# A fused Fourier-mixing and SwiGLU kernel: PSUM banks and work buffers handed out by the build-time planner, a table of unit kinds, and gates seeded by ScalarE

## The chip, the cores and the metric

The kernel runs on one core of one Trainium2 chip. The metric is device microseconds of one execution. A core has four engines that compute: TensorE (PE in the profile, its weight loads PEld), VectorE (DVE), ScalarE (ACT) and GpSimd (POOL). SyncE (SP) issues most of the transfers. Each engine runs its own list of instructions in order, and semaphores tie the lists together.

## The reference: what is computed

The input `x` has 8 sequences of 3008 rows and 256 columns. Its two-dimensional Fourier transform is taken (over rows, then over columns), the real part is kept, and each of the 24064 rows goes through a SwiGLU block with 1536 hidden columns:

```python
X = np.fft.fft(x, axis=1); X = np.fft.fft(X, axis=2); x = X.real
g = x @ w_gate                       # 256 -> 1536
silu = g * (1.0 / (1.0 + np.exp(-g)))
val = x @ w_val
return (silu * val) @ w_out          # 1536 -> 256
```

## The kernel before, in words

**Symmetry.** The transform of a real sequence at row M-k mirrors that at row k. So the kernel works on half of the rows, 12032 of them, as columns of two matrices: an even part P (tile `Pt`) and an odd part Q (`Qt`). For a column, the gate of row k is `Wp·P + Wq·Q` and that of its mirror row is `Wp·P - Wq·Q`; the same holds for the value. The transform over the 256 columns is folded into the weights (`Wp`, `Wq`), so only the transform over rows is done on data: GpSimd folds the loaded rows of a sequence (lines 158 to 182), TensorE multiplies them by tables of sines and cosines (`transform_op`), ScalarE copies one result out (`od`), and VectorE adds and subtracts to fill `Pt` and `Qt` (line 1345).

**Tiles and units.** The columns are cut into 24 tiles, most of them 512 wide (`wide`). A unit is a tile and one of 12 blocks of 128 hidden columns, so there are 288 units. For each unit, the gate and the value of the plus row and of the mirror row are formed in two PSUM banks, one for `g` and one for `v`, and turned into two products, `hp` (plus) and `hm` (mirror), in bf16. There are several kinds of unit:

- *Whole* units (18, in the first tiles): TensorE forms plus with `Wp·P + Wq·Q`, and then adds `Wm·Q` with `Wm = -2·Wq`, so that the same bank holds the mirror. That is three matmuls each for gate and value. Silu is ScalarE's, both products are VectorE's (`whole_a`, `whole_b`).
- *Ordinary* units: the gate as above in three matmuls, but the value in two. The value's even part is taken out of the bank after the first matmul (`es`); after the second one the bank holds the plus value, and VectorE makes the mirror as `2·es - v` (line 1124). The Q part lacks a term in its first row, and a copy of that row is spread over all partitions by two transfers per tile (`br`, `bc`). VectorE adds it, times a weight per partition (`w0`), while it takes the even part out (line 1063).
- *Seeded* values (`SEED`): ScalarE writes `bc` times `w0` into the bank before the first matmul (line 1012), the matmuls add to it, ScalarE copies the even part out (line 1061), and the last matmul uses `Wm` (by then rescaled to `-Wq`) in place of `Wq`.
- *Split* gates (`GATE`): the gate too is done in two matmuls, with the even part by VectorE (line 1042) and the mirror by VectorE (line 1102).
- *Pool* products (`POOL_END`): ScalarE copies the value out of the bank (line 1140) and GpSimd multiplies (line 1143), in place of VectorE (line 1134).

GpSimd multiplies the mirrors of two units at a time, from a buffer `sv` that holds silu and value side by side (line 1131). When a tile's 12 units are done, its `hp` and `hm` are multiplied with `Wo` during the next tile (`OWork`, 96 matmuls of 256 columns for a full tile), ScalarE copies each pair of results into an `ev` buffer (line 1186), and SP stores it.

**What sets the order.** Nothing in the steady part is written in its final order. Each piece of work is handed to `Sched.add` with its engine, an estimated duration, what it reads and writes, and the buffers that it opens. `Sched.run` then plays the engines forward: at each step it takes, within a window per engine, the piece that can start first by those estimates, and at the end it emits all instructions in that order. Buffers come from pools: PSUM 3 banks for `g`, 3 for `v`, 2 for output and transforms; in SBUF 3 each for `sp`, `sg` and `ev`, 2 each for `sv`, `es` and `od`. A pool hands out its buffers in the order in which they are asked for. The estimates before are, for instance:

```python
def pe_us(n):   return (n + 6) / 2400
def act_us(n):  return n / 1200 + 0.055
def dve_us(n):  return n / 960 + 0.072
```

Of the kernel before, what the change touches and what calls it, by code (L numbers as in the profile page):

```python
# [12 lines left out]
F32 = mybir.dt.float32  # L13
# [14 lines left out]

@with_exitstack
def kernel(
# [47 lines left out]
    odp = ctx.enter_context(tc.tile_pool(name="od", bufs=2))  # L80
# [3 lines left out]
    ctx.enter_context(tc.manual_schedule())  # L84

    Wp = const.tile([P, 2, Dff], BF16, name="Wp")
# [135 lines left out]
    SC = tq.tile([P, 2, 2, 2, D], F32, name="SC")  # L222
    SA = tp.tile([P, 2, 4, 2, D], F32, name="SA")
# [472 lines left out]
    sgp = ctx.enter_context(tc.tile_pool(name="sg", bufs=3))  # L696
    spp = ctx.enter_context(tc.tile_pool(name="sp", bufs=3))
    svp = ctx.enter_context(tc.tile_pool(name="sv", bufs=2))
    esp = ctx.enter_context(tc.tile_pool(name="es", bufs=2))
    brp = ctx.enter_context(tc.tile_pool(name="br", bufs=1))  # L700
    bcp = ctx.enter_context(tc.tile_pool(name="bc", bufs=2))
    evp = ctx.enter_context(tc.tile_pool(name="evO", bufs=3))
# [26 lines left out]

    ROW_GAP = 1  # L730
# [4 lines left out]
    ES_BUFS = 2  # L735
    SP_BUFS = 3
    SG_BUFS = 3
    EV_BUFS = 3
    W_PE = 2.0
    W_ACT = 2  # L740
    W_DVE = 3
    W_POOL = 6.0
    SH_SEED = -0.5
    SH_EG = 0.5
    SH_SP = 0.0
    SH_ES = 0.5
    SH_GM = 0.0
    SH_SM = 0.0
    SH_VM = 0.0
    SH_VAL = 0.0  # L750
    SH_HP = 1
    SH_HM = -0.5
    SH_EV = 0.5
    SH_FOLD = -2
    SH_OD = 0.0
    SH_PUT = -1
    GRP = 4
    WM_ACT = ((1, 0), (1, 1))
    class Op:
        __slots__ = ("eng", "dur", "lat", "fn", "at", "n", "deps", "owners", "new", "start", "end", "users")  # L760

    LAG = {"DMA": 0.0, "PE": 0.20, "ACT": 0.17, "DVE": 0.15, "POOL": 0.12, "SP": 0.0}
    BUFS = {"g": 3, "v": 3, "o": 2, "sp": SP_BUFS, "sv": 2, "es": ES_BUFS, "sg": SG_BUFS, "ev": EV_BUFS, "od": 2, "h": 2, "bc": 2, "br": 1, "pq": 5, "cp": 2,
            "fc": 1, "st": 3}
    WINDOW = {"PE": W_PE, "ACT": W_ACT, "DVE": W_DVE, "POOL": W_POOL, "SP": 3.0, "DMA": 1e9}
    PSUM = ("g", "v", "o")

    class Sched:

        def __init__(self):  # L770
            self.ops = []
            self.wr, self.rd = {}, {}
            self.live = {p: [] for p in BUFS}
            self.clock = 0.0

# [3 lines left out]
        def add(self, eng, dur, fn, r=(), w=(), new=(), lat=None, shift=0.0):  # L779
            o = Op()  # L780
            o.eng, o.dur, o.fn, o.n = eng, dur, fn, len(self.ops)
            o.lat = LAG[eng] if lat is None else lat
            o.at = self.clock + shift
            if eng == "PE":
                self.clock += dur
            o.new, o.deps, o.owners = list(new), set(), set()
            for k in r:
# [4 lines left out]
                if k[0][0] in PSUM:  # L792
                    o.deps.update(x for x in same if self.ops[x].eng != eng)
                same.append(o.n)
            for k in w:
# [4 lines left out]
                self.wr[k] = o.n  # L800
            o.deps.discard(o.n)
# [3 lines left out]
        def run(self, begin):  # L805
            ops = self.ops
            last, queue = {}, {p: [] for p in BUFS}
            for o in ops:
                for w_ in o.owners:
                    if w_[0] in BUFS:  # L810
                        last.setdefault(w_, set()).add(o.n)
                for w_ in o.new:
                    if w_ not in queue[w_[0]] and w_ not in self.live[w_[0]]:
                        queue[w_[0]].append(w_)
            free = {p: [0.0] * (BUFS[p] - len(self.live[p])) for p in BUFS}
            owned = {w_ for p in BUFS for w_ in self.live[p]}
# [3 lines left out]
            for l in todo.values():  # L820
                l.sort(key=lambda o: (o.at, o.n))
            t_eng = {e: begin.get(e, 0.0) for e in todo}
# [3 lines left out]
            for o in ops:  # L826
                o.end = None

            def ready(o):
                at = 0.0  # L830
                for d in o.deps:
                    x = ops[d]
                    if x.end is None:
                        return None
                    at = max(at, x.end + (x.lat if x.eng != o.eng or x.eng == "SP" else 0.0 if x.eng == "PE" else 0.03))
                for w_ in o.new:
# [3 lines left out]
                    if queue[p][0] != w_ or not free[p]:  # L840
                        return None
                    at = max(at, min(free[p]))
                return at

            while left:
                best = None
                floor = min(l[0].at for l in todo.values() if l)
                for e, l in todo.items():
                    if not l:
                        continue  # L850
                    pick = None
                    for o in l[:60]:
                        if o.at > l[0].at + WINDOW[e]:
# [4 lines left out]
                        s = max(at, t_eng[e], lanes[0] if e == "SP" else 0.0)  # L858
                        if pick is None or s < pick[0] - 0.01:
                            pick = (s, o)  # L860
                        if s <= t_eng[e]:
# [717 lines left out]
```

## Time and profile before

| | |
|---|---|
| three runs | 612.43, 613.17, 614.85 us; median 613.17 |
| span of the profiled execution, first to last instruction | 610.2 us |
| the profiled execution's own time | not listed; its span lies 3.0 us under the median of the runs and 2.2 under the fastest |
| granted TensorE clock | 1.000 |
| busy: PE, DVE, ACT, POOL | 601.1, 580.9, 525.3, 473.8 us |
| HBM traffic | 29.43 MB read, 24.65 MB written |

The groups that the change touches, each with its count, busy time and mean duration from the page:

```profile
L1131 POOL TENSOR_TENSOR hm<-sv 128x1024 bf16<-128x1024 f32 (+2 forms) x135 | 251.3, 1862 | 111.7 <-ACT sv L1110 61.6
L1134 DVE TENSOR_TENSOR hp<-sp,v 128x512 bf16<-128x512 f32 (+2 forms) x264 | 177.4, 672 | 5.6 <-ACT sp L1107 3.9
L1012 ACT ACTIVATE v<-bc,w 128x512 f32<-128x512 bf16 (+2 forms) x126 | 87.4, 694 | 0.2
L1042 DVE SCALAR_TENSOR_TENSOR sg<-bc,w,g 128x512 f32<-128x512 bf16 (+2 forms) x65 | 47.6, 732 | 1.2 <-ACT sg L975 0.7
```

How to read it: after the line and the engine come the operation, what it writes and reads, and its count; then the busy time in microseconds and the mean of one in nanoseconds; then the time that the engine had been idle before it, and what ended that. An instruction's duration overlaps the start of the next one on the same engine, so durations add up to more than the engine's time. `(+2 forms)` says that tiles of other widths are in the group.

### The profile page before, as it was taken

How to read it: one execution, taken by the hardware profiler on the slowest of the kernel's cores; microseconds unless marked ns; L12 is line 12 of the kernel's file. 1: busy time of each engine (PE TensorE's matmuls, PEld its weight loads, DVE VectorE, ACT ScalarE, POOL GpSimd, SP SyncE). 2: the span in 40 equal slices, each digit the busy share in tenths (PEclk: the TensorE clock that was granted, in tenths of full speed). 3: DMA queues.
4: the chain of work that ended last, by engine and by line, in shares of the span. 5: the costliest groups of instructions: out<-in, count | busy, mean ns of one | idle time of the engine just before them, and what ended most of it. 6: DMA issues, size and time to landing. Idle time of an engine off the chain costs nothing.

```text
span 610.2 us, 12592 instructions
## 1 busy us (share of the span) xinstructions
PE 601.1 (99%) x4088; PEld 396.9 (65%) x4088; DVE 580.9 (95%) x1073; ACT 525.3 (86%) x1003; POOL 473.8 (78%) x442
## 2 busy tenths in 40 slices
PE   8999999999999999999999999999999999999997
PEld 6555666666666666666666666666666666666686
DVE  8999899999999999999999999999999999999992
ACT  7686567899989889888999989998898988999994
POOL 8879999999697999987987869867886444446652
PEclk9999999999999999999999999999999999999999
DMA  9947446446317223463154113144211111111112
GB/s 227 144 100 136 127 114 176 118 137 149 107 45 164 70 65 120 121 142 116 45 118 116 54 45 97 53 100 120 62 54 43 52 55 52 48 43 55 59 53 79
DMA packets 50737, 57.71 MB, mean 95 GB/s; under 512 B 7257, under 2 KB 37725, under 8 KB 50671
## 3 DMA queue, kind: packets, MB, share of 16 engines
q1 hardware_dynamic: 47016, 53.78, 33.6%
q0 software_dynamic: 3216, 2.36, 2.8%
q10 hardware_dynamic: 438, 0.77, 0.4%
q8 instruction: 32, 0.52, 0.4%
q14 instruction: 35, 0.28, 0.2%
HBM read 29.43 MB, written 24.65 MB: 89 GB/s over the span
## 4 chain that ended last, share of the span: by engine, by line
PE 78%; DVE 8%; ACT 6%; issue 3%; POOL 2%; DMA 2%; ACTq 0%; POOLq 0%
PE o L1180 34%; PE g L940 22%; PE v L940 17%; ACT sv L1110 2%; PE o L1328 2%; DVE sv L1124 2%; PE g L1328 2%; DVE hp L1134 2%; DMA XA<-in_moe_w_val_dram 2%; ACT sp L1038 1%; ACT sp L1107 1%; DVE sg L1042 1%; DVE Qt L1345 1%; POOL EOA L485 1%; PE v L1180 1%
## 5 line engine op out<-in xcount | busy, mean ns | idle before, releaser
L1131 POOL TENSOR_TENSOR hm<-sv 128x1024 bf16<-128x1024 f32 (+2 forms) x135 | 251.3, 1862 | 111.7 <-ACT sv L1110 61.6
L1124 DVE SCALAR_TENSOR_TENSOR sv<-es,v 128x512 f32<-128x512 f32 (+2 forms) x270 | 181.0, 672 | 2.5 <-PE v L940 1.9
L1134 DVE TENSOR_TENSOR hp<-sp,v 128x512 bf16<-128x512 f32 (+2 forms) x264 | 177.4, 672 | 5.6 <-ACT sp L1107 3.9
L1180 PE MATMUL o<-Wo,hm 128*128 128x256 bf16 (+1 forms) x1128 | 166.0, 273 | 0.0
L1180 PE MATMUL o<-Wo,hp 128*128 128x256 bf16 (+1 forms) x1104 | 165.2, 273 | 0.0
L1038 ACT ACTIVATE sp<-g 128x512 f32<-128x512 f32 (+2 forms) x205 | 124.0, 605 | 32.9 <-PE g L940 29.9
L1180 PEld LDWEIGHTS <-hm 128*128 128x128 bf16 (+2 forms) x1140 | 112.0, 98 | 61.4 <-issue 0.2
L1180 PEld LDWEIGHTS <-hp 128*128 128x128 bf16 (+2 forms) x1140 | 112.0, 98 | 61.2 <-issue 3.5
L1110 ACT ACTIVATE sv<-g 128x512 f32<-128x512 f32 (+2 forms) x205 | 134.2, 657 | 5.5 <-PE g L940 3.5
L940 PE MATMUL v<-Pt,Wp 128*128 128x512 bf16 (+2 forms) x288 | 107.9, 375 | 0.3 <-DVE hm L998 0.3
L940 PE MATMUL g<-Pt,Wp 128*128 128x512 bf16 (+2 forms) x288 | 107.9, 375 | 0.0
L940 PE MATMUL g<-Qt,Wq 128*128 128x512 bf16 (+2 forms) x288 | 107.7, 375 | 0.0
L1063 DVE SCALAR_TENSOR_TENSOR es<-bc,w,v 128x512 f32<-128x512 bf16 (+2 forms) x144 | 105.3, 733 | 1.2 <-PE v L940 0.8
L1012 ACT ACTIVATE v<-bc,w 128x512 f32<-128x512 bf16 (+2 forms) x126 | 87.4, 694 | 0.2
L940 PE MATMUL g<-Qt,Wm 128*128 128x512 bf16 (+2 forms) x223 | 83.5, 374 | 0.7 <-ACT sp L1038 0.2
L1061 ACT COPY es<-v 128x512 f32<-128x512 f32 (+2 forms) x126 | 73.7, 585 | 1.7 <-PE v L940 1.0
L940 PEld LDWEIGHTS <-Wp 128*128 128x128 bf16 x576 | 56.3, 98 | 26.5 <-issue 2.0
L940 PE MATMUL v<-Qt,Wq 128*128 128x512 bf16 (+2 forms) x162 | 60.7, 375 | 1.6 <-DVE es L1063 1.6
L940 PEld LDWEIGHTS <-Wq 128*128 128x128 bf16 x450 | 44.0, 98 | 22.8 <-issue 0.8
L1186 ACT COPY ev<-o 128x512 f32<-128x512 f32 x89 | 53.8, 604 | 3.8 <-PE o L1180 2.7
L940 PE MATMUL v<-Qt,Wm 128*128 128x512 bf16 (+2 forms) x144 | 53.9, 374 | 0.1
L1042 DVE SCALAR_TENSOR_TENSOR sg<-bc,w,g 128x512 f32<-128x512 bf16 (+2 forms) x65 | 47.6, 732 | 1.2 <-ACT sg L975 0.7
(198 smaller groups left out, 688.0 us busy)
## 6 DMA issues: line engine op xcount, KB each, us to landing
out_dram<-ev SPq DMA_DIRECT2D x96, 128.0 KB
XA<-in_x_dram SPq DMA_DIRECT2D x30, 256.0 KB
XA<-in_x_dram SPq DMA_DIRECT2D x112, 64.0 KB
XC<-in_x_dram SPq DMA_DIRECT2D x30, 120.0 KB
XC<-in_x_dram SPq DMA_DIRECT2D x105, 32.0 KB
bc<-br SPq DMA_DIRECT2D x21, 128.0 KB
St<-Fc SPq DMA_DIRECT2D x14, 128.5 KB
out_dram<-ev SPq DMA_DIRECT2D x12, 120.0 KB
```

The source lines that it names most:

```text
L940: nc.tensor.matmul(ps[:, :n], Wt[:, gv, fs], src[:, :n], start=start, stop=stop, skip_group_check=True)
L1012: nc.scalar.activation(T_[kv][:, :w], bc[t][:, :w], AF.Copy, scale=w0[:, 1, f:f + 1])
L1038: nc.scalar.activation(T_[ksp][:, :w], T_[kg][:, :w], AF.Silu)
L1042: nc.vector.scalar_tensor_tensor(T_[keg][:, :w], bc[t][:, :w], w0[:, 0, f:f + 1], T_[kg][:, :w], op0=Alu.mult, op1=Alu.add)
L1061: nc.scalar.copy(T_[kes][:, :w], T_[kv][:, :w])
L1063: nc.vector.scalar_tensor_tensor(T_[kes][:, :w], bc[t][:, :w], w0[:, 1, f:f + 1], T_[kv][:, :w], op0=Alu.mult, op1=Alu.add)
L1110: nc.scalar.activation(sv()[:, f % 2, w - 1::-1, 1], T_[kgm if by_dve else kg][:, :w], AF.Silu)
L1124: nc.vector.scalar_tensor_tensor(sv()[:, f % 2, w - 1::-1, 0], T_[kes][:, :w], 2.0, T_[kv][:, :w], op0=Alu.mult, op1=Alu.subtract)
L1131: nc.gpsimd.tensor_tensor(hts_(t)[1][:, f - 1:f + 1, :w], sv()[:, :, :w, 1], sv()[:, :, :w, 0], op=Alu.mult)
L1134: nc.vector.tensor_tensor(hts_(t)[0][:, f, :wp], T_[ksp][:, :wp], T_[kv][:, :wp], op=Alu.mult)
L1180: nc.tensor.matmul(st["ps"][:n, j, :], hts[t][minus][:, f, c:c + n], Wo[:, f, :], start=(f == 0), stop=(f == nF - 1))
L1186: nc.scalar.copy(ev[:, 0:len(pair), :], st["ps"][:, 0:len(pair), :])
```

## The change

Four things change; the opening part of the kernel, the loads, the folds, the transforms, the output matmuls and the stores keep their work.

1. *Banks.* PSUM is one tile of 8 banks (`PS`). In the opening part three small rings deal out the same banks as the pools did. In the steady part every user, gate, value, output or transform, asks for a bank, and `Sched.run` picks one (`choose`). [...]
2. *Work buffers.* The pools `sg`, `sp`, `es`, `ev` and `od` (13 buffers) become 11 single buffers for any use, and `sv` two double ones (`ANY`); the planner picks. Five of the eleven and both double ones lie on memory that the opening part still uses, and are counted as taken for 14 us (`EARLY`).
3. *The planner.* Its windows, shifts and estimates are new numbers. An operation now has two durations: until its engine is free, and until others see the result (`TAIL`, `SEM`).
4. *Kinds.* A table gives each unit its gate (0 TensorE, 1 VectorE, 2 seeded by ScalarE), its value (0 whole, 1 VectorE, 2 seeded) and its product (D VectorE, P GpSimd). No gate in it is of kind 1, 82 are of kind 2; of the values 72 are seeded, 200 are VectorE's and 16 are whole; 58 products are GpSimd's. A seeded gate takes the same steps as a seeded value: ScalarE seeds the bank and copies the even part out, VectorE doubles and subtracts for the mirror. Its last matmul uses a new copy of weights, `Wg`, which VectorE makes once.

Counts in the built programs, before and after:

| | before | after |
|---|---|---|
| unit matmuls | 1393 | 1374 |
| ScalarE seeds (L1012; L1059 after) | 126 | 154 |
| ScalarE copies of even parts (L1061; L1066) | 126 | 154 |
| ScalarE copies of values for GpSimd (L1140; L1100) | 6 | 58 |
| VectorE even parts, gate and value (L1042, L1063; L1069) | 65 + 144 | 200 |
| VectorE gate mirrors (L1102; L1123) | 65 | 82 |
| VectorE value mirrors (L1124; L1137) | 270 | 272 |
| VectorE plus products (L978, L1134; L1107) | 282 | 230 |
| VectorE mirror products (L998; L1131) | 18 | 16 |
| GpSimd plus products (L1143; L1103) | 6 | 58 |
| GpSimd mirror products (L1131; L1144) | 135 | 136 |

The diff, cut to its core:

```diff
+EARLY = {**{("Q", i): 14.0 for i in range(2)}, **{("S", i): 14.0 for i in range(6, 11)}}
+KINDS = [
+    "000000000000 000000000000 DDDDDDDDDDDD",
+    "000000000000 001111001111 DDDDDDDDDDDD",
+    "000000000000 111111111111 DDDDDDDDDDDD",
+    "022200000220 122211112111 DDDDDDDDPPDD",
+    "000000020000 121121122112 DDPDDDDDDDDD",
+    "020202000200 222111121112 DDDDDDPDDDDD",
...
-    psG = ctx.enter_context(tc.tile_pool(name="psG", bufs=3, space=bass.MemoryType.PSUM))
-    psV = ctx.enter_context(tc.tile_pool(name="psV", bufs=3, space=bass.MemoryType.PSUM))
-    psO = ctx.enter_context(tc.tile_pool(name="psO", bufs=2, space=bass.MemoryType.PSUM))
+    PS = psp.tile([P, 8, T], F32, name="ps")
+    psG, psV, psO = Ring(0, 1, 2), Ring(3, 4, 5), Ring(6, 7)
+    Wg = const.tile([P, 1, Dff], BF16, name="Wg")
...
-    LAG = {"DMA": 0.0, "PE": 0.20, "ACT": 0.17, "DVE": 0.15, "POOL": 0.12, "SP": 0.0}
-    BUFS = {"g": 3, "v": 3, "o": 2, "sp": SP_BUFS, "sv": 2, "es": ES_BUFS, "sg": SG_BUFS, "ev": EV_BUFS, "od": 2, "h": 2, "bc": 2, "br": 1, "pq": 5, "cp": 2,
+    SEM = {"PE": 0.052, "ACT": 0.036, "DVE": 0.036, "POOL": 0.10, "SP": 0.06, "DMA": 0.0}
+    TAIL = {"PE": 0.163, "ACT": 0.118, "DVE": 0.08, "POOL": 0.02, "SP": 0.0, "DMA": 0.0}
+    FIFO = {"h": 2, "bc": 2, "br": 1, "pq": 5, "cp": 2, "fc": 1, "st": 3}
+    ANY = {"B": 8, "S": NS, "Q": NQ}
...
+            def choose(w_, e):
+                p = w_[0]
+                best = None
+                need = self.bits.get(w_, (0, 0))
+                for s in slots[p]:
+                    if p == "B" and need[0] and s[1] < need[0]:
+                        continue
+                    t = slot_time(s, e)
+                    waste = s[1] if p == "B" and not need[0] else 0
+                    k = (max(t, t_eng[e]), waste, t, s[2])
+                    if best is None or k < best[0]:
+                        best = (k, t, s)
+                return best
...
-    def act_us(n):
-        return n / 1200 + 0.055
+    def act_us(n, ptr=0, sbuf=0):
+        return n / 1200 + (0.094 if sbuf else 0.063) + 0.12 * ptr
...
-    SEED, SEED_END = (4, 5, 6, 8, 9, 11), (1, 3, 5, 7, 9, 11)
-    POOL, POOL_END = (), (6, 8)
-    GATE, GATE_END = (4, 8, 9), (3, 7, 9)
+    GATES, VALUES, PRODUCTS = kinds(nT, nF, t_end)
...
+            for gv, kind, k, cat in ((0, self.G, self.g, "seedg"), (1, self.V, self.v, "seedv")):
+                if kind != "2":
+                    continue
+                def fn(gv=gv, k=k):
+                    nc.scalar.activation(bank(k)[:, :self.wp], bc[self.t][:, :self.wp], AF.Copy, scale=w0[:, gv, self.f:self.f + 1])
...
+                S.add("PE", pe_us(wp), lambda: mm(bank(g), Wg if G == "2" else Wq, 0, u, self.src(1), wp, False, True), ...
...
+        if i == 2 * nF:
+            S.add("DVE", 0.5, lambda: vts(Wg[:, 0], Wm[:, 0], scalar1=-0.5, scalar2=None, op0=Alu.mult), w=[(("Wg",), 0)])
```

More of the change, by code (lines that the diff above doesn't have):

```diff
@@ L800, in add @@
                 self.wr[k] = o.n
+            for k in after:
+                o.deps.update(self.rd.get(k, ()))
             o.deps.discard(o.n)
@@ L1191, in store, with evict @@
-        def store(self, st, jj, p0, cnt, r0, step):
-            nc.sync.dma_start(out=rows(r0, cnt, step), in_=st["ev"][p0:p0 + cnt, jj, :])
-        def stores(self, pair, t):
-            return [(jj, p0, cnt, r0, step) for jj, (mi, cc, nn) in enumerate(pair)
+        def evict(self, ko, ke, two):
+            n = len(two)
+            if all(q[2] == P for q in two):
+                nc.scalar.copy(work(ke)[:, 0:n * D], bank(ko)[:, 0:n * D])
+            else:
+                for jj, q in enumerate(two):
+                    nc.scalar.copy(work(ke)[:q[2], jj * D:(jj + 1) * D], bank(ko)[:q[2], jj * D:(jj + 1) * D])
@@ L1196, in stores, with store @@
+        def store(self, ke, jj, p0, cnt, r0, step):
+            nc.sync.dma_start(out=rows(r0, cnt, step), in_=work(ke)[p0:p0 + cnt, jj * D:(jj + 1) * D])
+        def stores(self, two, t):
+            return [(jj, p0, cnt, r0, step) for jj, (mi, cc, nn) in enumerate(two)
                     for p0, cnt, r0, step in row_pieces(t0[t] + (width(t) - cc - nn if mi else cc), nn, mi)]
@@ L1479, in all_rows @@
         return fn
+    T_ = {}
     for t_ in (0, 1):
@@ L1491 @@
     owork = None
+    U = [Unit(u) for u in units]
     for i, u in enumerate(units):
@@ L1544 @@
     owork.run(len(owork.steps))
[L1545 to L1546 removed]
+    U[-1].b()
+    owork = OWork(prev[0])
     owork.run(len(owork.steps))
[L1548 removed]
+    S.run(BEGIN, EARLY)
 _INS = ['x', 'moe_w_gate', 'moe_w_val', 'moe_w_out']
```

658 lines of the change are left out of this document (303 added, 355 removed).

## The prediction

> **What bounds the kernel now.** I read the page's busy shares and chain, then the busy time by stage, then the waits, then a few microseconds of the timeline for the real pace of each engine. The page:
>
> ```profile
> span 610.2 us, 12592 instructions
> PE 601.1 (99%) x4088; PEld 396.9 (65%) x4088; DVE 580.9 (95%) x1073; ACT 525.3 (86%) x1003; POOL 473.8 (78%) x442
> PE 78%; DVE 8%; ACT 6%; issue 3%; POOL 2%; DMA 2%; ACTq 0%; POOLq 0%
> ```
>
> The reader sees a TensorE that is hardly ever idle, a VectorE close behind, and a chain that runs mostly through TensorE. Matmuls overlap in the trace, so "busy" alone proves little. The table by stage (in the columns: length, then PE, PEld, DVE, ACT, POOL busy) cuts the span at the first unit matmul (22.49), at tile 3 (98.26) and at the last unit matmul (598.41):
>
> ```profile
> 0.00:22.50 22.50, 20.20 (x149) 14.19 (x150) 19.61 (x68) 13.87 (x23) 17.57 (x39) 1.00 0.85 189
> 22.50:98.30 75.80, 72.93 (x465) 43.40 (x463) 72.33 (x130) 51.80 (x98) 70.73 (x87) 1.00 0.62 129
> 98.30:350.00 251.70, 251.56 (x1704) 166.23 (x1704) 246.94 (x442) 228.40 (x434) 220.36 (x194) 1.00 0.42 109
> 350.00:475.00 125.00, 124.79 (x844) 81.97 (x842) 122.59 (x226) 113.46 (x215) 97.64 (x85) 1.00 0.25 70
> 475.00:598.70 123.70, 123.58 (x865) 84.16 (x864) 118.57 (x212) 115.18 (x230) 66.22 (x39) 1.00 0.18 53
> ```
>
> From 98.3 to 598.7 (500.4 us, the steady stage) DVE is busy 488.1 and ACT 457.0; POOL thins out. The timeline tells the pace: the step from one start to the next, while the engine never idles (columns: start, duration).
>
> ```profile
> 431.51 0.38 PE L940 MATMUL v<-Pt,Wp 128*128 128x512 bf16 x1
> 431.72 0.38 PE L940 MATMUL g<-Qt,Wq 128*128 128x512 bf16 x1
> 431.94 0.38 PE L940 MATMUL v<-Qt,Wm 128*128 128x512 bf16 x1
> ...
> 430.32 0.69 ACT L1012 ACTIVATE v<-bc,w 128x512 f32<-128x512 bf16 x1
> 430.95 0.58 ACT L1061 COPY es<-v 128x512 f32<-128x512 f32 x1
> 431.43 0.58 ACT L1186 COPY ev<-o 128x512 f32<-128x512 f32 x1
> ...
> 433.43 0.60 ACT L1107 ACTIVATE sp<-g 128x512 f32<-128x512 f32 x1 [0.92 <-DVE sg L1102]
> 433.92 0.67 ACT L1110 ACTIVATE sv<-sg 128x512 f32<-128x512 f32 x1
> 434.48 0.57 ACT L1038 ACTIVATE sp<-g 128x512 f32<-128x512 f32 x1
> ...
> 432.06 0.74 DVE L1042 SCALAR_TENSOR_TENSOR sg<-bc,w,g 128x512 f32<-128x512 bf16 x1
> 432.71 0.68 DVE L1102 SCALAR_TENSOR_TENSOR sg<-sg,g 128x512 f32<-128x512 f32 x1
> 433.31 0.68 DVE L1124 SCALAR_TENSOR_TENSOR sv<-es,v 128x512 f32<-128x512 f32 x1
> ```
>
> So a 512-column matmul really costs 0.216, a ScalarE seed 0.62, a ScalarE copy 0.48, a Silu 0.49 from PSUM and 0.56 when its input is in SBUF, a VectorE operation 0.60, or 0.65 with the row and the pointer as inputs. Summing every matmul from 22.5 on at this pace gives 577.1 us up to TensorE's end at 606.7: of 584.2 us only 7.1 are stalls, 5.2 of them before 98.3 and 1.9 after. TensorE is the bound, VectorE is within some 4% of being one. The waits agree: the long ones are POOL's and ACT's own, the ones that stop TensorE are small.
>
> ```profile
> POOL hm L1131 <- ACT sv L1110: 61.6, 44, 3.6
> ACT sp L1038 <- PE g L940: 29.9, 39, 2.5
> PE v L940 <- DVE es L1063: 1.6, 3, 0.9
> ```
>
> **The change part by part**, with counts from the instruction lists of the two built programs.
>
> *TensorE.* The unit matmuls go from 1393 to 1374: 82 gates instead of 65 get the mirror from another engine, and 16 whole units instead of 18. 19 x 0.216 = 4.1 us less, all from tile 3 on; the 2280 output matmuls and the transforms stay. This is the only sure gain. [...]
>
> *VectorE.* Even parts formed there (gate and value): 65 + 144 = 209 become 200, -9 x 0.65 = -5.9. Its plain operations (mirror by doubling, mirror value, products): 635 become 600, -35 x 0.60 = -21.0, mostly because 52 products go to POOL. One new scaling that makes Wg, taken at 0.65 from the nearest row (between 0.3, a narrow put, and 1.6, its 1536 columns at the 512-column pace). Sum -26: busy 488 becomes 462 of the stage. It was hidden under TensorE, so this gives nothing by itself; it takes away the second limit.
>
> *ScalarE.* Seeds 126 to 154, and as many copies of seeded halves; values copied for POOL 6 to 58; 17 more mirrored Silus read SBUF. 28 x 0.62 + 28 x 0.48 + 52 x 0.48 + 17 x 0.07 = 17.4 + 13.4 + 25.0 + 1.2 = 57 us, all from tile 3 on. Two sums for the stage: the upper is what it was busy, 457, less the overhang of about 0.1 at each of some 125 idle spots, plus 57: about 500. The lower prices each instruction at the step it has when its successor waits for nothing: about 489. TensorE's stage after its saving is 496. So ScalarE, with 43 us to spare before, now has between +7 and -4. I take the lower, because the upper still holds short waits that hide inside a duration and would vanish on a full engine.
>
> *GpSimd.* One group's row:
>
> ```profile
> L1143 POOL TENSOR_TENSOR hp<-sp,sg x6: 880/1277/1282, 550.5 to 595.8; 128x512 bf16<-128x512 f32 x4, 128x328 bf16<-128x328 f32 x2
> ```
>
> 52 more such products x 1.28 = 67 us, spread over tiles 3 to 23. Where folds still run (350 to 475) it was busy 97.6 of 125; three more per 24 us make about 117. Hidden, with little left. [...]
>
> *Banks.* Eight PSUM banks for anyone instead of 3, 3 and 2; TensorE's waits on its own results fall from 111 rows to 1. As the stalls are 7.1 in all, this can give at most that. Of the 5.2 before tile 3, where units wait for VectorE (54 and 74 us) and weights arrive by DMA (29 and 32 us), it may win all or none; I take half, 2.6.
>
> *Buffers.* Eleven single slots serve Silus, even parts, values, transforms and output rows. Before, only ScalarE's evictions reused a buffer that a store was reading; now VectorE waits for DMA in 207 rows instead of 41. What queues behind such a wait is VectorE's whole order: products that free banks, then TensorE. The planner counts 0.45 + 2.6 us for a store; in the trace a quiet store's packets are through 1.1 to 3.2 us after issue, but it is issued a median 1.2 us after its eviction ends, and up to 8.2 us before 250 us. So a reuse that was planned without slack is about 1 us late. Some 90 reuses follow a store. Bounds: none of them tight, 0; or one in ten (my guess), 9 us. I take 0, since any free slot may be picked: eleven for all uses, where thirteen buffers in five pools served before. Both ends go into the range. SP issues the same loads and stores.
>
> *Opening and end.* 22.5 and 11.5 us, the same work in the same order.
>
> Sum: 22.5 + (75.8 - 2.6) + (500.4 - 4.1 + 1.5) + 11.5 = 605.0 us of span. The steady stage keeps its 1.9 us of stalls, and I let it lose 1.5 more, for two engines are now full. The median of the runs is 613.17, 3.0 above the span, so 608.0.
>
> **The rivals.**
>
> *ScalarE idles as VectorE did; no change.* The nearly full VectorE sat idle 12.4 us of the steady stage. Add that to ScalarE's lower sum: 489 + 12.4 = 501, and the early stage stays: 22.5 + 75.8 + 501 + 11.5 + 3.0 = 614. For it: in-order engines that feed each other. Against: VectorE's idling was slack, not need.
>
> *ScalarE becomes the bound; slower.* With the middle of its two sums, 495 + 12.4 = 507: 22.5 + 75.8 + 507 + 11.5 + 3.0 = 620. It decides from the point where its work and idling pass 500.4. Place: tiles 3, 5, 7, 10, 12 and 16, where eight or nine seeds stand in one tile of 24 us. Against: a heavy tile can borrow from the next one through the slots.
>
> *GpSimd or a store is late; slower.* One 1.85 us operation late in each of six fold tiles (11 us), or the 9 us of late slots: 617 to 619.
>
> [...]
>
> *The change does nothing beyond its matmuls:* 609.
>
> **How the numbers follow.** The runs spread over 0.4%, so 0.5%, 3.1 us, is about what can be told from no change. TensorE stays the bound, 602 (no stall at all: 599 + 3.0) to 610: 0.55, the last rival within it. ScalarE or the port giving the gain back, 610 to 616: 0.22. Slower by ScalarE 0.16, by GpSimd or stores 0.07. The range runs from 602.5 to 618, where it leaves out about half of the slower cases.
>
> **What would show it.** Right: the steady stage at 496 to 499, ACT busy above 490 with few idle spots, DVE's busy time down by 25, matmul steps still 0.216 with stalls below 6 us. Wrong: TensorE waiting for a ScalarE seed or copy in tiles 5, 7 and 12; VectorE or ScalarE waiting for out_dram stores; GpSimd without idle time from 350 to 475 and mirror values waiting for it. A steady stage of 501 or more would break the forecast.

## The result, and the profile after it

The changed kernel is slower: 633.35 us in the median of 4 runs (628.90 to 638.76) against 613.47 for the kernel before in the same session, a ratio of 1.0303 (95% interval 1.0257 to 1.0349). The longest of the four runs lies 1.6% above the fastest and counts as slow: the ratio leaves it out, and the median of the other three, 631.46, stands for the changed kernel from here on. The forecast was 608, with a range up to 618. The profiled execution took 631.5 us, with a span of 629.7.

The page of the changed kernel, its span, busy shares and chain:

```profile
span 629.7 us, 12646 instructions
PE 607.7 (97%) x4069; PEld 395.8 (63%) x4069; DVE 559.1 (89%) x1030; ACT 572.3 (91%) x1111; POOL 537.1 (85%) x495
PE 62%; DMA 16%; POOL 8%; ACT 5%; issue 3%; SPq 3%; DVE 2%; ACTq 0%; POOLq 0%; DVEq 0%
```

The work moved the way that was forecast: VectorE lost 22 us of busy time, ScalarE gained 47, GpSimd 63. But TensorE's share of the chain fell from 78% to 62%, and transfers, which held 2% of it, now hold 16%. The table by stage (columns as before: length, then PE, PEld, DVE, ACT, POOL busy, granted clock), cut at the same places, and then single stretches of 100 us:

```profile
22.50:98.30 75.80, 70.13 (x445) 41.48 (x444) 68.46 (x118) 51.34 (x96) 67.90 (x82) 1.00 0.56 120
98.30:350.00 251.70, 244.58 (x1610) 158.06 (x1610) 226.15 (x407) 240.04 (x464) 229.23 (x205) 0.99 0.43 108
350.00:475.00 125.00, 121.38 (x806) 78.08 (x804) 108.83 (x196) 120.88 (x234) 114.23 (x96) 1.00 0.27 70
475.00:618.00 143.00, 142.99 (x993) 96.63 (x991) 134.18 (x240) 142.27 (x289) 105.61 (x77) 1.00 0.17 52
...
200.00:300.00 100.00, 96.20 (x636) 62.42 (x635) 90.24 (x168) 93.05 (x180) 92.16 (x83) 0.98 0.47 115
300.00:400.00 100.00, 99.67 (x667) 64.87 (x666) 93.82 (x163) 99.51 (x194) 93.79 (x80) 1.00 0.29 77
400.00:500.00 100.00, 96.70 (x640) 62.08 (x639) 86.61 (x154) 95.95 (x186) 91.00 (x79) 1.00 0.27 70
500.00:600.00 100.00, 99.99 (x676) 65.72 (x675) 95.49 (x167) 99.81 (x196) 69.61 (x44) 1.00 0.17 51
```

Read the last four lines against each other. From 300 to 400 and from 500 to 600 ScalarE is full (99.5 and 99.8 of 100) and TensorE loses almost nothing. Where TensorE does lose, from 200 to 300 and 400 to 500, ScalarE is *less* busy: something stops both. The waits of the changed kernel (who waited for what, us in total, times, longest) name it:

```profile
ACT wk1s L1310 <- DMA out_dram<-wk1s: 5.0, 1, 5.0
DVE wk5s L1123 <- DMA out_dram<-wk5s: 3.2, 1, 3.2
ACT wk5s L1084 <- DMA out_dram<-wk5s: 3.1, 1, 3.1
ACT wk3s L1126 <- DMA out_dram<-wk3s: 2.7, 1, 2.7
...
PE ps L1003 <- ACT wk1s L1310: 2.8, 1, 2.8
PE ps L1003 <- ACT wk3s L1126: 2.7, 1, 2.7
PE ps L1003 <- ACT wk5s L1084: 2.5, 1, 2.5
```

ScalarE and VectorE wait for *stores*: they want to write into a single slot that an output row is still being read from. In sum 17.4 us (ScalarE 14.2 in 9 waits, VectorE 3.2 in one); before it was 0.1. Each of ScalarE's three longest waits comes back as a wait of TensorE for that same instruction. One of them in full, from the timeline (SP's issues, then ScalarE, then TensorE):

```profile
199.64 5.93 SPq L181 DMA_DIRECT2D XA<-in_x_dram  x12
...
206.23 1.23 SPq L1183 DMA_DIRECT2D out_dram<-wk5s  x2
207.98 2.96 SPq L181 DMA_DIRECT2D XA<-in_x_dram  x4
...
213.11 0.60 ACT L1084 ACTIVATE wk5s<-ps 128x512 f32<-128x512 f32 x1 [3.08 <-DMA out_dram<-wk5s]
...
210.66 0.59 PE L1003 MATMUL ps<-Qt,Wm 128*128 128x512 bf16 x2
213.76 0.38 PE L1003 MATMUL ps<-Qt,Wm 128*128 128x512 bf16 x1 [2.51 <-ACT wk5s L1084]
```

ScalarE had copied the output row into wk5s at 199.6 (0.65 us). SP was at that moment beginning twelve loads of the next sequence and came to the store only at 206.2; the store landed just before 213.1, 5.6 us after its last issue ended. The row held its slot for 12.8 us after it was written. The planner counts 0.45 + 2.6 us from the moment at which, in its plan, SP gets to the store.

A measure for all that follows is TensorE's time without work: from the first unit matmul to TensorE's end, less all matmuls at the step that they have at full clock (0.216 us for 512 columns). Before: 606.7 - 22.5 - 577.1 = 7.1 us. After: 626.2 - 22.2 - 573.3 = 30.7. The span grew by 19.5 us: matmul work -3.8, time without work +23.6, the opening 0.3 shorter, the end the same. So the gain in matmul work came as forecast and was lost six times over.

### The profile page after: what moved, and what is told of

Read it like the earlier page. It is cut to its first block, busy times and chain, and to the rows that moved or that the text cites. A ratio compares the mean times of both kernels' runs of the same rounds, so it can differ in the third digit from the quotient of the medians.

```text
span 629.7 us, 12646 instructions
## 1 busy us (share of the span) xinstructions
PE 607.7 (97%) x4069; PEld 395.8 (63%) x4069; DVE 559.1 (89%) x1030; ACT 572.3 (91%) x1111; POOL 537.1 (85%) x495
## 4 chain that ended last, share of the span: by engine, by line
PE 62%; DMA 16%; POOL 8%; ACT 5%; issue 3%; SPq 3%; DVE 2%; ACTq 0%; POOLq 0%; DVEq 0%
PE ps L1003 31%; PE ps L1171 27%; DMA XA<-in_x_dram 7%; POOL hm L1144 3%; PE ps L1299 3%; DMA XA<-in_moe_w_val_dram 2%; DMA out_dram<-wk5s 1%; POOL SDf L207 1%; DMA br<-Qt 1%; DMA XC<-in_x_dram 1%; ACT ps L1059 1%; SPq L1183 1%; DMA out_dram<-wk1s 1%; DMA out_dram<-wk8s 1%; SPq L181 1%
## 5 line engine op out<-in xcount | busy, mean ns | idle before, releaser
L1003 PE MATMUL ps<-Pt,Wp 128*128 128x512 bf16 (+2 forms) x576 | 206.1, 376 | 8.5 <-ACT wk1s L1310 2.8
L1171 PE MATMUL ps<-Wo,hp 128*128 128x256 bf16 (+2 forms) x1140 | 167.5, 273 | 0.1
L1171 PE MATMUL ps<-Wo,hm 128*128 128x256 bf16 (+2 forms) x1140 | 166.5, 272 | 0.4 <-ACT wk0s L1177 0.3
L1003 PE MATMUL ps<-Qt,Wq 128*128 128x512 bf16 (+2 forms) x422 | 155.2, 377 | 1.9 <-DVE wk1s L1069 1.2
L1144 POOL TENSOR_TENSOR hm<-sv1q 128x1024 bf16<-128x1024 f32 (+2 forms) x68 | 126.6, 1862 | 25.5 <-ACT sv1q L1115 22.9
L1144 POOL TENSOR_TENSOR hm<-sv0q 128x1024 bf16<-128x1024 f32 (+2 forms) x68 | 126.6, 1862 | 20.8 <-ACT sv0q L1115 17.4
L1059 ACT ACTIVATE ps<-bc,w 128x512 f32<-128x512 bf16 (+2 forms) x154 | 112.4, 738 | 1.2 <-DVE hp L1107 0.3
L1003 PE MATMUL ps<-Qt,Wm 128*128 128x512 bf16 (+2 forms) x294 | 105.2, 376 | 2.6 <-ACT wk5s L1084 2.5
L1115 ACT ACTIVATE sv0q<-ps 128x512 f32<-128x512 f32 (+2 forms) x101 | 68.8, 686 | 3.5 <-PE ps L1003 2.0
L1115 ACT ACTIVATE sv1q<-ps 128x512 f32<-128x512 f32 (+2 forms) x89 | 61.4, 697 | 3.7 <-PE ps L1003 3.6
L217 POOL TENSOR_TENSOR Af<-EOf 128x516 f32<-128x516 f32 (+1 forms) x22 | 24.2, 1101 | 0.6
L1069 DVE SCALAR_TENSOR_TENSOR wk2s<-bc,w,ps 128x512 f32<-128x512 bf16 (+1 forms) x30 | 22.3, 742 | 0.0
```

Of the source, the lines that this page charges most:

```text
L217: tt(Af[r], EOf[r, :, 0:2, :], EOf[r, :, 2:4, :], op=Alu.add)
L1003: nc.tensor.matmul(ps[:, :n], Wt[:, gv, fs], src[:, :n], start=start, stop=stop, skip_group_check=True)
L1059: nc.scalar.activation(bank(k)[:, :self.wp], bc[self.t][:, :self.wp], AF.Copy, scale=w0[:, gv, self.f:self.f + 1])
L1069: nc.vector.scalar_tensor_tensor(work(e)[:, :self.wp], bc[self.t][:, :self.wp], w0[:, gv, self.f:self.f + 1], bank(k)[:, :self.wp], op0=Al ...
L1115: return lambda: nc.scalar.activation(self.silu(self.sm, w), src()[:, :w], AF.Silu)
L1144: lambda: nc.gpsimd.tensor_tensor(tiles_of(t)[1][:, f - 1:f + 1, :w], pair(self.vm)[:, :, :w, 1], pair(self.vm)[:, :, :w, 0], op=Alu.mult),
```

## The experiments

Each kernel was timed against the kernel before on the same chip and in the same session (there 612.2 to 612.8 us). The changed kernel was not run again in those sessions, so kernels are best compared by their ratios. "Without work" and "store waits" (ScalarE plus VectorE) come from the one profiled execution, which can lie a few us off its kernel's median: these kernels spread by 0.6 to 1.6%, the kernel before by 0.2 to 0.7%. "Without work" also holds what TensorE lost at half clock (last section), at most 1.7 us for each piece of 3.4 us. There are two such pieces in "after", "store counted 4.0 us", "another order" and "gate seeds on TensorE" (mean granted clock 0.994 to 0.995), one in "table of before, store 6.0", "repair" and "store 6.0, rows 1 us later" (0.997), and none in the others (1.000).

| kernel | median us | ratio, 95% interval | without work | store waits |
|---|---|---|---|---|
| before | 613.47 | | 7.1 | 0.1 |
| after | 631.46 | 1.0303 [1.0257, 1.0349] | 30.7 | 17.4 |
| store counted 6.0 us | 615.91 | 1.0077 [1.0046, 1.0107] | 14.5 | 0.5 |
| store counted 4.0 us | 625.79 | 1.0220 [1.0170, 1.0269] | 24.2 | 8.8 |
| output rows in slots of their own | 617.99 | 1.0077 [1.0051, 1.0102] | 17.2 | 1.2 |
| later loads left out | 614.12 | 1.0036 [1.0020, 1.0051] | 12.6 | 0 |
| another order, nothing else | 627.84 | 1.0237 [1.0179, 1.0294] | 27.1 | 10.8 |
| table of before | 622.97 | 1.0169 [1.0135, 1.0203] | 14.7 | 3.8 |
| table of before, store 6.0 | 618.92 | 1.0099 [1.0080, 1.0118] | 17.4 | 2.3 |
| gate seeds on TensorE | 635.31 | 1.0388 [1.0336, 1.0441] | 15.3 | 3.2 |
| GpSimd's new products on VectorE | 626.52 | 1.0232 [1.0194, 1.0269] | 23.5 | 8.7 |
| repair | 616.96 | 1.0061 [1.0038, 1.0085] | 17.9 | 0.4 |
| repair, from the table of before | 616.70 | 1.0074 [1.0048, 1.0100] | 13.1 | 0 |
| store 6.0, rows 1 us later | 621.53 | 1.0138 [1.0112, 1.0165] | 19.6 | 2.1 |

### A store counted at 6.0 us

```diff
-  S.add("SP", 0.45, lambda ...: self.store(ke, *args), r=[ke], lat=2.6)
+  S.add("SP", 0.45, lambda ...: self.store(ke, *args), r=[ke], lat=6.0)
```

> One number of the planner: a store is counted to hold its buffer 6.0 us after its issue instead of 2.6; instructions and shapes stay, the order on TensorE too. Theory S (work buffers are handed on while a store still reads them, 14.2 us of such waits on ScalarE and 3.2 on VectorE in the changed kernel): these waits fall below 4 us, TensorE's stalls after 22.5 us go from 30 to about 12, the time from 633 to 612-618. Rival F (ScalarE and GpSimd are simply too full): stays within 3 us of 633. Rival T (the plan is tight everywhere, and any late thing costs the same): falls by at most 6 us, and other waits take the place of those.

One number in the planner, not one instruction more or less, and the matmuls in the same order: 631.46 became 615.91. The traces show more: ScalarE, VectorE, GpSimd and SP also run through the same lines on the same shapes in the same order as in the changed kernel. What differs is which slot each result goes into. The waits for stores and rows that are left:

```profile
DVE wk0s L1069 <- DMA bc<-br: 2.9, 1, 2.9
ACT ps L1059 <- DMA bc<-br: 1.9, 1, 1.9
DVE wk1s L1069 <- DMA bc<-br: 1.7, 1, 1.7
DVE wk5s L1069 <- DMA bc<-br: 0.7, 1, 0.7
DVE wk10s L1123 <- DMA out_dram<-wk10s: 0.5, 1, 0.5
```

All store waits but one are gone, and with them 16.2 of the 23.6 us of time without work. ScalarE is as full as before the edit (here from 350 to 475 and from 475 to 602):

```profile
350.00:475.00 125.00, 123.75 (x817) 80.49 (x830) 112.03 (x203) 124.45 (x241) 119.12 (x102) 1.00 0.27 72
475.00:602.00 127.00, 126.26 (x870) 85.98 (x883) 118.39 (x213) 126.33 (x258) 90.22 (x62) 1.00 0.17 52
```

so "ScalarE is the bound" does not explain the loss. (Some 60 matmul records are missing from this trace and from those of most kernels below, so their PE columns are a little low.)

### Output rows in slots of their own

```diff
-  ANY = {"B": 8, "S": NS, "Q": NQ}
+  ANY = {"B": 8, "S": NS - 3, "Q": NQ, "E": 3}
-  ko, ke = (("B", "o", (t, i)), 0), (("S", "ev", (t, i)), 0)
+  ko, ke = (("B", "o", (t, i)), 0), (("E", "ev", (t, i)), 0)
```

> Three of the eleven single buffers are for output rows alone, as before the change; eight serve the rest; the store's estimate stays 2.6 us. Theory S: VectorE and all of ScalarE but its evictions no longer wait for a store; waits for out_dram below 4 us in all and only before evictions; 612-618 us. Rival F: 630 or more. Rival B (eight buffers are too few for the rest): waits of ScalarE for VectorE and of VectorE for ScalarE grow instead, 625-640.

The store is still counted at 2.6 us, but a slot whose row is late can now stop only the next output row. Of the 90-odd reuses that follow a store, those that write within 6 us of the end of its issue fall from 58 to 5 (to 5 as well with the store at 6.0). This kernel has eight slots for the rest instead of eleven and still gains 14 us (ratio 1.0077 instead of 1.0303): what cost time was that slots of output rows were shared while the planner believed in a short store.

### No loads behind the first ones

```diff
   for what, k, fn in loads[:n]:
+      if what[1] >= (2 if what[0] == "A" else 3):
+          fn = lambda: None
```

> The changed kernel without the loads of x from the third sequence on (the folds work on old rows, so most of the output is of other data; all other work and the whole order stay). Theory S in its sharper form (stores are late because SP and the transfer engines are busy with loads): the stalls between 100 and 450 us vanish, those before 60 us stay, 610-617 us. If stores are late by themselves: 628 or more. Rival F: 630 or more.

No wait for a store is left, at the planner's 2.6 us, though 45 of the 90 reuses still come within 6 us of the end of the store's issue. So the stores are late because of the loads. How: from the moment an output row is written to the start of its store's issue, up to 450 us, it takes a median of 1.3 us in the changed kernel, but 6.0 in the upper quartile, 10.7 in the upper tenth and 16.0 at most. Without the loads that is 0.4, 0.9, 3.4 and 9.1. In the kernel before, with the loads, it was 0.7, 1.5, 3.0 and 9.0. The same loads and stores stand in SP's list in another order. And the loads themselves come late and close together, because SP's list stops at a load whose target GpSimd's folds have not given back; the waits of SP's queue in the changed kernel:

```profile
SPq L181 <- POOL EOf L208: 16.9, 4, 8.3
SPq L190 <- POOL EOf L208: 5.7, 2, 2.9
```

22.6 us, where the kernel before had 3.4 for the lines that do the same.

### Another order of the same work

```diff
-  hp=6.081
+  hp=5.081
```

> Control: one shift of the planner (plus products, 6.081 to 5.081) that changes no estimate, only the order and with it which buffers are reused when. Theory S: the tight reuses stay as frequent, so 626-640 us with the large stalls at other places. If the loss hangs on a few unlucky spots of this one order: below 622.

This offset only reorders the same operations. The loss stays, at other places (the largest stalls of TensorE end at 168.5, 293.7 and 435.7 instead of 98.7, 213.8 and 441.5). So another order by itself did not bring the gain back (only this one was tried, and the store at 6.0 keeps the order anyway). But some 4 us lie between these two orders of one program, and differences of that size between kernels of different order mean little.

### A store at 4.0 us

> The changed kernel with a store counted at 4.0 us in place of 2.6 (6.0 gave 615.9 us, 2.6 gives 633). The matmuls keep their order. Theory S (the loss is the part of a store's life that the planner does not count) has a dose in it: the transfers land up to 6 us after their issue and the issues are themselves late behind loads, so 4.0 us covers part of them; TensorE's time without work lies between the 14.5 us of 6.0 and the 30.7 us of 2.6, at 16 to 24 us, store waits of 2 to 8 us are left, and the time is 617 to 626 us. Rival (any other order of the other engines would have been as good): no dose, the time as at 2.6 or as at 6.0.

Store waits of 8.8 us and 24.2 us without work: between the two, and nearer to 2.6 than I thought. The order is again that of the changed kernel, on every engine and on SP, and the reuses within 6 us of the end of the store's issue are 31, between 58 and 5. In this trace one store landed 5.6 us after its issue ended (at 207.6), and its issue can itself be late.

### The table of the kernel before, under the new planner

```diff
-    "022200000220 122211112111 DDDDDDDDPPDD",
+    "000010001100 111122212212 DDDDDDDDDDDD",
```

(One line is shown. Every tile from 2 on gets the line of the kernel before; tile 2 and the last three have lines of their own there. The planner's offset `eg`, for the even parts of gates on VectorE, goes from -31.963 to 8.0; no unit of the changed kernel uses it.)

> The changed kernel with the kernel before's table of unit kinds (1393 unit matmuls again in place of 1374, the gate seeds back on VectorE and TensorE, ScalarE relieved of some 57 instructions) but with the new planner, its shared single slots and its 2.6 us for a store. Theory S (slots handed on while a store still reads them cost most of the loss, whatever the table): store waits of 5 to 15 us in sum come back on ScalarE and VectorE, TensorE gets 4.1 us more work, and the time is 622 to 634 us. Rival T (the new table fills ScalarE, and that is what makes the late stores bite and the small waits appear): ScalarE has slack again, the store waits are absorbed, and the time is 612 to 617 us.

> The kernel before's table under the new planner as above, with a store counted at 6.0 us, so that no slot is handed on too early. With the new table this setting gave 615.9 us, with 14.5 us of TensorE time without work after its first unit matmul against 7.1 us in the kernel before. Theory T2 (the 7 us left over are ScalarE's, because the new table gives it more than it can do without lateness): the time without work falls to 7 to 10 us and, with 4.1 us more matmul work, the time is 612 to 616 us. Rival P (the 7 us left over come from the new planner's tight order and shared slots, with any table): 13 to 18 us stay without work and the time is 618 to 623 us.

With the old table the slots are shared just as much and counted just as short, and 42 reuses instead of 58 fall within 6 us of the end of the store's issue. Yet store waits shrink from 17.4 to 3.8 us and the time without work from 30.7 to 14.7. Stretches of this kernel's table by stage:

```profile
200.00:300.00 100.00, 99.61 (x676) 65.34 (x674) 98.38 (x183) 90.33 (x171) 87.27 (x77) 1.00 0.38 107
300.00:400.00 100.00, 100.00 (x672) 65.15 (x670) 98.63 (x173) 91.52 (x173) 82.50 (x71) 1.00 0.29 78
400.00:500.00 100.00, 99.89 (x674) 65.46 (x672) 98.30 (x176) 90.13 (x172) 73.85 (x63) 1.00 0.25 70
500.00:600.00 100.00, 100.00 (x693) 67.34 (x691) 95.54 (x174) 92.81 (x186) 52.83 (x31) 1.00 0.17 51
```

ScalarE has 9% of its time free and TensorE loses little (3.4 us without work from 200 to 600). So neither theory stood as I put it: early reuse alone does not cost 25 us, and a full ScalarE alone does not either (with the store at 6.0).

What the longer count brings with the old table depends on where one looks. In the profiled executions it brought nothing: 14.7 and 17.4 us without work. But that of the first kernel was the fastest of its four runs (619.8), and that of the second the slowest (621.8), with two long waits of VectorE for rows (9.5 us together, against one of 4.8) and a piece at half clock. The runs say otherwise: ratios of 1.0169 and 1.0099, with intervals that do not overlap, and the same order of instructions in both. The short count costs about 4 us with the old table and about 14 with the new one (1.0303 and 1.0077). So, by the runs, the new table makes the short count some three times as costly, but the count costs time without that table too.

Whether it is ScalarE's free time that hides the late stores is not shown by this pair. The old table also takes 52 products from GpSimd, and stores are issued earlier: from the row written to the start of the issue, the upper quartile is 2.8 us instead of 6.0. That 13 to 18 us stay even with ScalarE relieved and stores counted long was the rival's forecast, and it held.

### The gate seeds back on TensorE

```diff
-    "022200000220 122211112111 DDDDDDDDPPDD",
+    "000000000000 122211112111 DDDDDDDDPPDD",
```

(One line is shown; all tiles from 3 on change in the same way.)

> The changed kernel with the 82 gate seeds that the new table gives to ScalarE done by TensorE instead, all else of the table kept, a store still counted at 2.6 us. It adds 82 unit matmuls of 0.216 us (17.7 us) to TensorE and takes some 50 us from ScalarE. Theory S x A (an early hand-on costs time only where ScalarE has no slack to absorb it): TensorE's time without work falls from 30.7 us to 8 to 16 us, and the time is 573.3 + 17.7 of matmul work + 22.3 before them + 5.3 behind them + 8 to 16 = 626 to 635 us. Rival (the early hand-on costs the same whatever ScalarE has to do): 25 to 32 us stay, and the time is 643 to 651 us.

82 matmuls more, 60 us less on ScalarE (512.2 busy instead of 572.3) and 38 less on VectorE, which no longer makes these gates' mirrors: 15.3 us without work instead of 30.7, of which 3.3 is one wait for weights at 32 us and about 2.9 the half clock that follows it. The time of 635.3 lies at the edge of what slack on ScalarE allowed and 8 us under the rival. So with the short count the seeds save 17.7 us of matmul work and cost 15.4 us of time without work. That they do so by taking ScalarE's slack fits, but this order also has fewer early reuses (26 of 90 instead of 58) and earlier stores (upper quartile 3.0 us instead of 6.0), so slack is not the only thing that changed.

### GpSimd's new products back on VectorE

```diff
-    "022200000220 122211112111 DDDDDDDDPPDD",
+    "022200000220 122211112111 DDDDDDDDDDDD",
```

(One line is shown; all tiles from 3 on change in the same way.)

> The changed kernel with all of the products that the new table gives to GpSimd back on VectorE, a store still counted at 2.6 us. In the trace of the changed kernel, loads of x on SyncE wait 22.6 us for GpSimd's folds and then go out in a burst, with the stores behind them. Theory G (GpSimd's 67 us more work is what makes folds, loads and so stores late): the store waits of ScalarE and VectorE fall from 17.4 us to under 6 us, and the time, with VectorE fuller, is 615 to 625 us. Rival N (GpSimd has no part in it, stores are late behind loads anyway and ScalarE has no slack): 10 to 20 us of store waits stay and the time is 628 to 642 us.

Between the two forecasts. SP's waits for folds fall from 22.6 to 10.1 us, store waits from 17.4 to 8.7, so about half of the lateness goes with GpSimd's extra work. Whether it goes because of it is less sure: with the gate seeds on TensorE, where GpSimd keeps all its products, SP's waits for folds also fall, to 15.9 us. And VectorE, now full (from 500 to 600 it is busy 99.8), costs TensorE time of its own:

```profile
500.00:600.00 100.00, 96.88 (x634) 62.54 (x643) 99.78 (x180) 90.18 (x175) 45.21 (x25) 1.00 0.17 50
```

TensorE loses some 6 us in that stretch, mostly in waits for ScalarE, and about half of ScalarE's own waits there are for VectorE.

### Two repairs and one more number

The numbers of the planner, written short:

```diff
-  lat=2.6 (store)   lat=2.6 (br)   lat=3.0 (bc)   LANE = 3.0   FOLD_US = (2.0, ...
+  lat=5.0 (store)   lat=3.6 (br)   lat=4.0 (bc)   LANE = 3.4   FOLD_US = (2.3, ...
+  if eng in ("ACT", "DVE", "POOL"):
+      o.dur *= 1.005
+      o.lat *= 1.005
```

The planner's offsets and the tables were chosen again for these numbers. (The last kernel has only the store at 6.0 and the first row transfer, `br`, at 3.6.) In the second of the two repairs, two units of tile 2 take the halved matrix `Wm` before it is halved, so their values are not the reference's; the instructions are as many as they would be.

> A repair of the changed kernel: the planner counts what the traces showed (a store 5.0 us in place of 2.6, the row transfers 3.6 and 4.0 in place of 2.6 and 3.0, a lane 3.4 in place of 3.0, the first step of a fold 2.3 in place of 2.0, every operation of ScalarE, VectorE and GpSimd 0.5% more), and its offsets and the table of kinds from tile 3 on were chosen again for these numbers; 1374 unit matmuls as in the changed kernel, 82 gate seeds on ScalarE. Theory (the loss is the hand-on of slots and rows that come too early in the plan): store waits under 2 us, the waits for bc rows under 3 us, 8 to 12 us of TensorE time without work, and 22.4 + 573.3 + 8 to 12 + 5.3 = 609 to 613 us, so no slower than the kernel before. Rival (a full ScalarE with lateness of its own always costs some 7 us more than the old pools did): 14 to 17 us without work and 615 to 618 us.

> The same counts in the planner, with a table that starts from that of the kernel before: 1383 unit matmuls, 18 gate seeds on ScalarE and 57 on VectorE, 29 pairs of products on GpSimd (the changed kernel 58), so ScalarE keeps about 10% of its time free. Theory S x A: 8 to 11 us of TensorE time without work, and 22.4 + 573.3 + 9 x 0.216 + 8 to 11 + 5.3 = 611 to 614 us. Rival (what is left over comes with the shared slots and banks whatever the planner counts): 14 to 17 us without work and 617 to 620 us.

> The changed kernel with a store counted at 6.0 us, and in addition the first of a tile's two row transfers at 3.6 us in place of 2.6, so that the planner hands the row out 1 us later. With 6.0 alone the waits for rows were 7.2 us on ScalarE and VectorE, TensorE was 14.5 us without work, and the time 615.9 us. Theory (what the planner counts too low is late on the chip, rows as well as stores): row waits of 2 to 5 us, 11 to 14 us without work, 612 to 615 us. Rival (rows are late because SyncE's list is behind, whatever they are counted at): row waits stay at 6 to 9 us, and the time is 615 to 619 us.

The store waits are gone in both repairs (0.4 and 0), and neither beats the kernel before. The first, at 616.96, lies where its rival said; of its 17.9 us without work, 3.7 are one wait for weights at 32 us and the half clock after it. The second, at 616.70 with 13.1 us, lies between its two forecasts, next to the rival's. The last kernel brought the waits for rows down from 7.2 to 2.8 us, as its theory said, and still took 621.5: in its new order one store of a slot held VectorE for 2.1 us at 105.8 and one row ScalarE for 2.2 us at 177. No kernel of this study is faster than the one before.

Where the rest stays, by the time without work in three stretches (the last 0.3 to 0.6 us of each kernel are left out):

| us without work | to 100 us | 100 to 200 | 200 to 600 |
|---|---|---|---|
| before | 5.5 | 0.2 | 1.7 |
| after | 9.2 | 6.1 | 15.4 |
| store 6.0 | 4.6 | 4.2 | 5.7 |
| table of before | 6.1 | 5.5 | 3.4 |

With the store at 6.0, 1.9 of the 4.2 us is one row transfer that ScalarE waits for at 173; the 5.7 are scattered waits, none over 0.4 us, the longest of them mostly for copies and Silus of ScalarE. That the new planner's orders, with any table, leave more of these than the old one's is measured; which of its numbers does it stays open.

## Why the prediction was wrong

*TensorE: right.* The matmul work fell by 3.8 us (573.3 against 577.1), 4.1 forecast, and the stalls went into the time one for one.

*VectorE, ScalarE, GpSimd: the sizes about right.* They changed by -22, +47 and +63 us of busy time; -26, +57 and +67 were forecast. ScalarE was indeed full with room for what it had to do: 99.8 of 100 busy with TensorE at 99.99 from 500 to 600. As the bound by itself, the rival of 620, it did not come.

*Banks: wrong, and small.* Half of the early 5.2 us was to vanish; to 100 us the time without work rose from 5.5 to 9.2, as a first store wait of 5.0 us fell into it. With the store at 6.0 it is 4.6.

*Buffers: the step that failed.* I bounded the term by 0 and 9 us and took 0, "since any free slot may be picked". It was 16.2 us: so much comes back with the store's length alone, in the same order on every engine. About 3.3 of them were lost to half clock (last section). Three things in that step were wrong. First, a free slot in the plan is not a free slot on the chip, and a planner that may pick any slot left little slack: 58 of 90 reuses came within 6 us of the end of the store's issue. I guessed one in ten late, by 1 us; it was 10 waits of 1.7 us on average. Second, the lateness was taken from the old trace, 1.2 us in the median and up to 8.2. "SP issues the same loads and stores" was true and not enough: their order was new, the loads waited longer for GpSimd's folds, and the wait from row to store went to 6.0 us in the upper quartile. Third, I priced a late slot and a full ScalarE as separate rivals, with a chance of 0.07 for the one. They are not separate: by the runs, the short count costs about 14 us with the new table and about 4 with the old one. That ScalarE's last 9% of slack, which I had counted as a saving, is what would have hidden the stores is the likely reason; the runs that relieved ScalarE also made the stores earlier, so it is not shown alone.

*Two full engines: too small.* The sum held 6.0 us of time without work (7.1 - 2.6 + 1.5); it was 30.7. Of the 24.7 us between, 16.2 are the stores. The rest lies mostly in the 1.5 us that I let the steady stage lose "for two engines are now full": with the store at 6.0 it lost 8.0 more than before from 100 us on (9.9 against 1.9). A full ScalarE does not explain it, as the table of before, with ScalarE 9% free, has 8.9 there. It comes with the new planner, and what in it does this stays open.

*GpSimd late: partly right.* It does not stop TensorE itself, as I had priced it; it gives its input back late (22.6 us of SP's waits instead of 3.4), so that loads bunch in front of the stores. Half of the lateness goes with its products, in the one order that was run.

*The port in the rivals' 0.22:* no run shows it. VectorE's busy time fell by 22 of the 26 us forecast (580.9 to 559.1), and in the changed kernel its operations step at 0.60 from 524.08 to 525.27, while a GpSimd product of 1.90 us that began at 523.70 runs.

*The rival "nothing beyond its matmuls", 609:* not even the repaired kernels reach it, as rows and small waits take the 3.8 us back.

## What to carry to other kernels

When buffers that a transfer reads are thrown into one pool with buffers that the engines hand to each other, count their hold from the moment of writing to the *landing*, at the slow end of what the trace shows, with the issuing queue's delay in it; a median was not enough here: the one estimate cost about 14 us with the new table and about 4 with the old. Before moving work to an engine "because it has 14% free", ask which lateness that free time is absorbing now: here a short estimate and a fuller table cost far more together than either alone, though whether by the lost slack was not shown. And a change that reorders a queue without adding to it can still change the delays in that queue: here the upper quartile of the wait from row to store went from 1.5 to 6.0 us.

## What the runs showed of the hardware

TensorE's granted clock fell to one half (0.50) in the middle of the changed kernel, for 3.41 us each at 98.5 and at 214.6. The stretches at full clock before, between and after them lasted 92.16, 112.64 and 413.01 us in this trace, which is 27, 33 and 121 times 3.413. The changed kernel's table, cut into pieces of that length (the clock is the third figure from the end, PE's busy time the second of the line):

```profile
95.09:98.51 3.42, 0.81 (x6) 0.48 (x5) 0.18 (x1) 0.34 (x1) 3.42 (x3) 1.00 0.53 126
98.51:101.92 3.41, 3.22 (x8) 1.13 (x8) 3.24 (x10) 3.41 (x7) 2.76 (x3) 0.50 0.87 151
211.15:214.56 3.41, 0.90 (x6) 0.48 (x5) 0.99 (x2) 1.45 (x4) 3.41 (x3) 1.00 0.79 151
214.56:217.98 3.42, 3.42 (x16) 2.10 (x15) 2.31 (x8) 2.57 (x6) 2.88 (x3) 0.50 1.04 223
436.43:439.84 3.41, 2.37 (x17) 1.50 (x16) 1.55 (x3) 1.68 (x4) 2.08 (x2) 1.00 1.03 271
439.84:443.25 3.41, 1.79 (x13) 1.23 (x13) 1.81 (x7) 2.44 (x5) 0.83 (x1) 1.00 0.20 65
443.25:446.66 3.41, 3.38 (x24) 2.03 (x23) 2.66 (x6) 3.38 (x8) 3.33 (x6) 1.00 0.00 0
```

The pieces in which TensorE was busy 0.81 and 0.90 us were followed by pieces at half clock, in which the 512-column matmuls stepped at 0.43 us instead of 0.216. The stall of 2.8 us that ended at 441.5 fell across two pieces, busy 2.37 and 1.79, and the clock stayed at 1.00. Over all kernels, ten pieces with 0.34 to 1.51 us of busy time were followed by half clock, and five (1.50, 1.55, 1.63, 1.74 and 1.79) were not. With the gate seeds on TensorE one such piece, busy 1.31 and ending at 31.0, stands before two pieces at half clock (0.95 in the mean from 22.5 to 98.3; with the repair, which has one there, 0.98). What decides the clock was not shown beyond these pieces. In the changed kernel the two stalls that lay mostly within one piece cost an estimated 1.6 and 1.7 us more, half of the 3.22 and 3.42 us that TensorE was busy in the pieces after them, and the one that was cut in two cost nothing more. Whether this is a part of why the changed kernel spreads by 1.6% from run to run stays open: its four runs, 628.90, 631.46, 635.24 and 638.76 us, had mean granted clocks of 0.992, 0.995, 0.989 and 0.992, which do not follow their times.
